# Layer A's Q and K turned by 32x32 block transposes on VectorE instead of 128x128 transposes on TensorE

## The chip, the cores and the metric

One of the eight cores of a Trainium2 chip runs the whole program. The metric is the device time of one execution in microseconds (us). Times of instructions come from the profiled execution. Engines are named as the profile names them: PE is TensorE's matrix multiply, PEld its weight load, DVE is VectorE, ACT is ScalarE, POOL is GpSimd, SP issues DMAs.

## The reference

Four layers in a row, A, B, A, B, on one sequence of 2048 rows of 512, each with a residual and a layer norm ahead of it. The two A layers have the same weights, so have the two B layers.

```python
def _A_ref(x, mem0, Wq, Wk, Wv, Wo, seg_len):      # H = 32 heads of 128, M = 8, seg_len = 32
    mem = mem0
    for s in range(n_seg):                          # 64 segments, one after the other
        h = jnp.concatenate([mem, xs], axis=1)      # 40 rows
        q, k, v = (einsum('btd,dhe->bhte', h, W) for W in (Wq, Wk, Wv))
        scores = einsum('bhqe,bhke->bhqk', q, k) * scale      # masked
        o = einsum('bhqk,bhke->bhqe', softmax(scores), v)
        o = einsum('bhte,hed->btd', o, Wo)
        mem = o[:, :M]                              # the next segment needs it
        outs.append(o[:, M:])
def _B_ref(x, wqkv, wo):                            # full softmax attention, 32 heads of 16, no mask
    ...
x = x + _A_ref(_layernorm(x), ...);  x = x + _B_ref(_layernorm(x), ...)
x = x + _A_ref(_layernorm(x), ...);  x = x + _B_ref(_layernorm(x), ...)
```

The 64 segments of a layer A are a chain, since each needs the memory rows that the one before it made. Layer B is a large amount of work without such a chain.

## The kernel before

**Order of the work.** The Python code that builds the program keeps a clock of its own for PE, ACT and DVE (class `Clock`) and puts TensorE's instructions in order by it: at each step the method `step` takes what can start first of three kinds of work. These are the steps of the present segment of layer A (from a list, `PLAN`, or `PLAN_PAIRS` where at least five units of B are due in the segment; `a_pick` looks at the first six steps left), units of layer B, and chains (layer norm, projections of B, output of B) with planned places `PLACE` and `B_PLACE`. The other engines take their instructions in the order in which a scheduler puts them. Each engine's queue is worked off in order.

**A segment of layer A.** It has 32 main rows (8 memory rows and 24 fresh ones); the 8 remaining fresh rows of four segments are gathered in `a_hX` and go through the projections once for four segments, by the chain in `ln_chunk`. A projection is split into two halves of sixteen heads (`rr`). For a half, `col_steps` issues sixteen matmuls (L737): the 32 rows of `a_hT` are the weights of a 32-column tile of the array, four column tiles stand side by side, each streams 512 columns of W, and the four results lie in the four quarters of a PSUM bank's partitions. Steps `Q0 Q1 K0 K1 V0 V1` are these. For Q and K the bank is copied to SBUF as bf16 (`a_qk`, through `evac`, on ACT or DVE, whichever the clock says ends first). The rows then lie on the partitions, and the scores need the head's 128 elements there. Steps `X0 X1` (Q) and `Y0 Y1` (K) do this turn: four 128x128 transposes on TensorE (L761) into a bank, and a copy of it to `a_QT` or `a_KT` (`evac16`, L335 on ACT, L337 on DVE). For the gathered rows, `turn` in `ln_chunk` does it for K and Q at once, eight transposes from `a_qkx` to `a_KX` and `a_QX`; GpSimd later copies their parts to `a_KT` and `a_QP`. `S0 S1` are the scores (L795, L801), the exponential on ACT (L805), and on DVE the sum, the reciprocal, the product and two 32x32 block transposes (L808 to L817). `P0 P1` or the halves `A`, `B` are the products with V (L824), evacuated to `a_OT`, and `W0` to `W3` the products with Wo (L854), after which DVE writes the next segment's memory rows (L978).

**A unit of layer B** (`emit_qk`, `pv_mm`) is four row-tiled score matmuls of 512 columns (L588), two exponentials on ACT, one of 1536 columns out of the three banks of `b_SX` (L590) and one of 512 out of a fourth bank (L593), and four column-tiled matmuls with V (L602). `b_SX` exists once. How many units go into a segment is the segment's quota: none while there is no backlog, 8 at most, and up to 13 in the last 16 segments. What is left of layer B when the last segment is done is worked off in the tail by `fill` (L473, and L476 on ACT, 1536 columns each).

**Tiling mode.** Matmuls over the full array, row-tiled ones (L588, L824) and column-tiled ones (L737, L795, L801, L602) alternate on TensorE; the builder's clock charges 0.104 us for a change from one to another.

Of the kernel before, what the change touches and what calls it, by code (L numbers as in the profile page):

```python
# [40 lines left out]
PLACE = (-2.0, -1.5, -1.4, -1.4, -1.3, -0.5, -0.4, -0.4, 3.8)  # L41
B_PLACE = (-2.7, -1.4, 0.4, 0.7, 1.7)
# [70 lines left out]
class Kern:  # L113
    def __init__(self, ctx, tc, T):
# [103 lines left out]
    def a_buffers(self, bp):  # L218
# [442 lines left out]
    def ln_chunk(self, A, ck):  # L661
# [30 lines left out]
        qk = {}  # L692

        def one(rr, w):
            def then(b, done):
                t = self.lnp.tile([128, 512], bf16, name="a_qkx", tag="t", bufs=4)
                b.free = self.evac(t[:], b.t[:], 512, done)
                qk[w] = (t, b.free)
            return self.col_steps((self.Wq, self.Wk)[w], lambda ft: self.hX[:, ft, :], rr, max(self.at["x"], self.w_at["QK"[w]]), then)

        def turn(rr):
            b, done = self.turn((qk[1], qk[0]))
            ps = b.h(8, 128)
            self.evac16(self.KX[:, rr].rearrange("p j t q -> p j (t q)"), ps[:, 0:4], 512, done)
            b.free = self.evac16(self.QX[:, 4 * rr:4 * rr + 4].rearrange("p t j q -> p t j q"), ps[:, 4:8].rearrange("p j (t q) -> p t j q", q=32), 512, done)
            if rr:
                self.at["X", ck] = b.free
            return b.free
# [41 lines left out]
    def stage(self, b, done):  # L750
        t = self.stp.tile([128, 512], bf16, name="a_qk")
        b.free = self.evac(t[:], b.t[:], 512, done)
        return t, b.free
# [957 lines left out]
```

## Time and profile before

| | |
|---|---|
| median of 3 runs | 3019.47 us (3016.03 to 3024.8) |
| span of the profiled execution, first to last instruction | 3016.9 us |
| what lies around that span, up to the median of the runs | 2.6 us |
| PE busy | 2793.8 us, 93% of the span |
| ACT busy | 2296.1 us, 76% |
| DVE busy | 1787.0 us, 59% |
| the transposes L761 | 2560 in all, 219.5 us of PE's busy time |

PE's busy time counts a matmul from its start to a modelled end, and matmuls overlap, so a busy PE is not PE at its peak. Where all of PE's instructions follow each other without a gap, the chain of waits gives the time that each group adds.

### The profile page before, as it was taken

How to read it: one execution, taken by the hardware profiler on the slowest of the kernel's cores; microseconds unless marked ns; L12 is line 12 of the kernel's file. 1: busy time of each engine (PE TensorE's matmuls, PEld its weight loads, DVE VectorE, ACT ScalarE, POOL GpSimd, SP SyncE). 2: the span in 40 equal slices, each digit the busy share in tenths (PEclk: the TensorE clock that was granted, in tenths of full speed). 3: DMA queues.
4: the chain of work that ended last, by engine and by line, in shares of the span. 5: the costliest groups of instructions: out<-in, count | busy, mean ns of one | idle time of the engine just before them, and what ended most of it. 6: DMA issues, size and time to landing. Idle time of an engine off the chain costs nothing.

```text
span 3016.9 us, 153258 instructions
## 1 busy us (share of the span) xinstructions
PE 2793.8 (93%) x68190; PEld 1702.6 (56%) x68190; DVE 1787.0 (59%) x4836; ACT 2296.1 (76%) x2816; POOL 661.3 (22%) x1165
## 2 busy tenths in 40 slices
PE   5999999999999999999999999999999999998897
PEld 3666565655555555555656655555556555554463
DVE  2344646476666766577766667767666666654302
ACT  2555767587788788667787777778778899899996
POOL 2222222222222222203212212222222122221110
PEclk9999999999999999999999999999999999999998
DMA  6112224243444446435434433544452544555340
GB/s 255 50 47 77 87 82 122 83 136 114 141 123 142 136 118 192 125 106 171 131 99 123 123 91 116 149 140 129 120 170 81 171 125 131 182 168 159 104 120 14
DMA packets 281282, 373.74 MB, mean 124 GB/s; under 512 B 74105, under 2 KB 202305, under 8 KB 279073
## 3 DMA queue, kind: packets, MB, share of 16 engines
q1 hardware_dynamic: 222096, 186.25, 21.9%
q0 software_dynamic: 55040, 168.68, 17.6%
q8 instruction: 535, 8.77, 1.2%
q10 hardware_dynamic: 3472, 8.91, 0.8%
q14 instruction: 139, 1.13, 0.1%
HBM read 260.06 MB, written 103.55 MB: 121 GB/s over the span
## 4 chain that ended last, share of the span: by engine, by line
PE 62%; ACT 14%; DVE 9%; issue 8%; DMA 6%; POOL 1%; SPq 0%; DVEq 0%; ACTq 0%; POOLq 0%
PE bank L737 23%; PE bank L854 12%; ACT b_pr L476 7%; PE b_SX L588 6%; PE b_oacc L602 6%; PE bank L761 4%; ACT b_pt L590 3%; PE bank L824 3%; DMA b_W<-in_B_wqkv_dram 2%; ACT b_pt L593 2%; PE bank L801 1%; PE bank L1237 1%; PE bank L1283 1%; DMA a_Wq<-in_A_Wq_dram 1%; DVE a_qk L326 1%
## 5 line engine op out<-in xcount | busy, mean ns | idle before, releaser
L590 ACT ACTIVATE b_pt<-b_SX 128x1536 bf16<-128x1536 f32 (+1 forms) x877 | 1270.9, 1449 | 384.3 <-PE bank L588 354.6
L593 ACT ACTIVATE b_pt<-bank 128x512 bf16<-128x512 f32 (+1 forms) x877 | 523.2, 597 | 0.6 <-PE bank L588 0.6
L854 PE MATMUL bank<-a_OT,a_Wo 128*128 128x40 bf16 x16384 | 482.0, 180 | 24.3 <-ACT a_OT L324 18.4
L854 PEld LDWEIGHTS <-a_Wo 128*128 128x128 bf16 x16384 | 449.4, 96 | 67.2 <-issue 58.7
L737 PEld LDWEIGHTS <-a_hT 128*32 128x32 bf16 x12288 | 298.0, 96 | 294.9 <-issue 38.5
L588 PE MATMUL b_SX<-b_q,b_k 32*128 32x256 bf16 (+3 forms) x3870 | 353.0, 313 | 21.1 <-ACT b_pt L590 13.8
L588 PE MATMUL bank<-b_q,b_k 32*128 32x512 bf16 (+3 forms) x1290 | 337.0, 312 | 8.4 <-DVE a_V L326 2.5
L602 PE MATMUL b_oacc<-b_pt,b_v 128*17 128x512 bf16 (+3 forms) x5160 | 322.9, 314 | 11.0 <-DVE b_ain L1070 4.3
L326 DVE CAST a_OT<-bank 128x160 bf16<-128x160 f32 x778 | 216.7, 316 | 127.9 <-PE bank L824 125.1
L737 PE MATMUL bank<-a_Wv,a_hT 128*32 128x512 bf16 x4096 | 285.4, 383 | 1.7 <-DVE b_O L1330 1.3
L326 DVE CAST a_qk<-bank 128x512 bf16<-128x512 f32 x338 | 229.5, 681 | 84.2 <-PE bank L737 79.6
L737 PE MATMUL bank<-a_Wk,a_hT 128*32 128x512 bf16 x4096 | 271.8, 382 | 5.3 <-DVE a_hT L978 5.1
L737 PE MATMUL bank<-a_Wq,a_hT 128*32 128x512 bf16 x4096 | 275.5, 381 | 0.7 <-DVE a_V L326 0.4
L476 ACT ACTIVATE b_pr<-b_S 128x1536 bf16<-128x1536 f32 x202 | 270.9, 1876 | 1.1 <-PE b_S L473 1.1
L588 PEld LDWEIGHTS <-b_k 32*128 32x128 bf16 x5160 | 119.2, 91 | 193.7 <-issue 156.0
L1055 POOL DMA_DIRECT2D b_A<-b_ain x176 | 96.2, 546 | 595.8 <-DVE b_ain L1070 403.1
L1070 DVE TENSOR_TENSOR b_ain<-b_oacc,b_ain 128x512 f32<-128x512 f32 (+1 forms) x244 | 165.6, 679 | 91.9 <-PE b_oacc L602 88.0
L602 PEld LDWEIGHTS <-b_v 128*17 128x17 bf16 x6432 | 117.2, 88 | 163.0 <-issue 125.1
L761 PE MATMUL bank<-c_ident,a_qk 128*128 128x128 bf16 x2048 | 179.9, 221 | 23.1 <-DVE a_qk L326 12.7
L824 PE MATMUL bank<-a_PT,a_V 32*128 32x40 bf16 x3472 | 181.0, 177 | 15.3 <-DVE chk L351 3.4
L761 PEld LDWEIGHTS <-a_qk 128*128 128x128 bf16 x2048 | 119.6, 98 | 123.6 <-DVE a_qk L326 49.9
L808 DVE TENSOR_REDUCE a_sm<-a_pn 128x5 f32<-128x200 bf16 x256 | 92.4, 361 | 161.3 <-ACT a_pn L805 157.6
(156 smaller groups left out, 4103.1 us busy)
## 6 DMA issues: line engine op xcount, KB each, us to landing
b_ain<-b_A SPq DMA_DIRECT2D x232, 256.0 KB
b_W<-in_B_wqkv_dram POOLq DMA_DIRECT2D x192, 256.0 KB, 4.0
b_A<-b_ain POOLq DMA_DIRECT2D x176, 256.0 KB, 3.0
b_q<-b_Q SPq DMA_DIRECT2D x252, 128.0 KB
b_k<-b_K SPq DMA_DIRECT2D x199, 128.0 KB
b_v<-b_V SPq DMA_DIRECT2D x306, 68.0 KB
b_A<-b_aout POOLq DMA_DIRECT2D x80, 128.0 KB, 2.8
a_rest<-a_vx POOLq DMA_DIRECT2D x64, 128.0 KB, 2.7
```

What stands on the lines that cost most here:

```text
L326: self.nc.vector.tensor_copy(dst, src)
L476: nc.scalar.activation(self.ring[:, s:s + n, :], self.sets[i][:, 0:n, :], ACT.Exp, scale=B_SCALE)
L588: nc.tensor.matmul(out[t][:, j * qw:(j + 1) * qw], lhsT=k[32 * t:32 * t + 32, kj * 128:(kj + 1) * 128], rhs=q[32 * t:32 * t + 32, j * u.ru ...
L590: nc.scalar.activation(pt[:, 0:NX, 0:w], self.SX[:, 0:NX, 0:w], ACT.Exp, scale=B_SCALE)
L593: nc.scalar.activation(pt[:, NX + i, 0:w], b.t[:, 0:w], ACT.Exp, scale=B_SCALE)
L602: self.nc.tensor.matmul(self.oacc[32 * t:32 * t + 17, j * step:j * step + qw], lhsT=u.v[:, kj, 17 * t:17 * t + 17], rhs=u.p[:, t, j * qw:( ...
L737: self.nc.tensor.matmul(b.t[32 * t:32 * t + 32, :], lhsT=lhsT(ft), rhs=W[:, ft, n * 512:(n + 1) * 512], start=(ft == 0), stop=(ft == 3), t ...
L761: self.nc.tensor.transpose(ps[:, 4 * i + j, :], x[:, 128 * j:128 * j + 128], self.ident[:])
L824: self.nc.tensor.matmul(ps[:, L * h4:L * h4 + L], lhsT=V[32 * t:32 * t + rows, st, h4 * DH:(h4 + 1) * DH], rhs=self.PT[32 * t:32 * t + row ...
L854: self.nc.tensor.matmul(ps[:, ft, :], lhsT=self.Wo[:, h, 128 * ft:128 * ft + 128], rhs=self.OT[:, h, :], start=(h == 0 and ft == 0), stop= ...
L1055: B.k.nc.gpsimd.dma_start(B.Acc_d[self.qc][self.hg][:, self.qo:self.qo + self.qw], acc[:, 0:self.qw])
L1070: nc.vector.tensor_tensor(acc[:, w], k.oacc[:, w], acc[:, w], ALU.add)
```

## The change

Q and K are no longer turned on TensorE. The projection streams W in another order of columns: a column tile now gets 32 of the 128 elements of each of the sixteen heads of its half, as sixteen runs of 32 columns that lie 128 columns apart (`Wt[:, ft, rr, :, t, :]`), where it got four whole heads as 512 columns in a row. In the bank, each 32x32 block is then one head's rows by 32 of its elements, in the quarter of the partitions where those elements belong. After the copy to `a_qk`, one `nc.vector.transpose` of 128x512 turns all 64 blocks in place of four TensorE transposes and the second copy out of PSUM. V and Wo keep their code.

```diff
-PLACE = (-2.0, -1.5, -1.4, -1.4, -1.3, -0.5, -0.4, -0.4, 3.8)
+PLACE = (-2.1, -1.6, -1.4, -1.1, -0.9, -0.5, -0.4)
...
-        self.QT = bp.tile([128, 2, 4, 4, MAIN], bf16, name="a_QT")
-        self.KT = bp.tile([128, 2, 4, 4, L], bf16, name="a_KT")
+        self.QT = bp.tile([128, 2, 16, MAIN], bf16, name="a_QT")
+        self.KT = bp.tile([128, 2, 16, L], bf16, name="a_KT")
...
         def one(rr, w):
             def then(b, done):
-                t = self.lnp.tile([128, 512], bf16, name="a_qkx", tag="t", bufs=4)
-                b.free = self.evac(t[:], b.t[:], 512, done)
-                qk[w] = (t, b.free)
...
-        def turn(rr):
-            b, done = self.turn((qk[1], qk[0]))
...
+                at = self.turn((self.QX, self.KX)[w][:, rr], b, done)
...
-    def col_steps(self, W, lhsT, rr, ready, then):
+    def col_steps(self, W, lhsT, rr, ready, then, turned=False):
         st = {}
+        Wt = W[:].rearrange("p f (r i t c) -> p f r i t c", r=2, t=4, c=32)
...
-                self.nc.tensor.matmul(b.t[32 * t:32 * t + 32, :], lhsT=lhsT(ft), rhs=W[:, ft, n * 512:(n + 1) * 512],
-                                      start=(ft == 0), stop=(ft == 3), tile_position=(0, 32 * t))
+                out, rhs = b.t[32 * t:32 * t + 32, :], W[:, ft, n * 512:(n + 1) * 512]
+                if turned:
+                    out, rhs = out.rearrange("p (i c) -> p i c", c=32), Wt[:, ft, rr, :, t, :]
+                self.nc.tensor.matmul(out, lhsT=lhsT(ft), rhs=rhs, start=(ft == 0), stop=(ft == 3), tile_position=(0, 32 * t))
...
-    def turn(self, xs):
-        b, at = self.take()
-        ps = b.h(8, 128)
-        for i, (x, _) in enumerate(xs):
-            for j in range(4):
-                self.nc.tensor.transpose(ps[:, 4 * i + j, :], x[:, 128 * j:128 * j + 128], self.ident[:])
+    def turn(self, dst, b, done):
+        x = self.stp.tile([128, 16, 32], bf16, name="a_qk")
+        b.free = self.evac(x[:].rearrange("p i c -> p (i c)"), b.t[:], 512, done)
+        self.nc.vector.transpose(dst, x[:])
+        return self.ck.ew("DVE", 512, b.free)
...
-    PLAN = "K0 Q0 P1 Q1 Y0 X0 S0 W1 K1 W0 Y1 V0 X1 W3 W2 V1 S1 P0".split()
-    PLAN_PAIRS = "W1 Q0 W3 V0 Y0 K0 A1 X0 S0 X1 V1 K1 Q1 B0 Y1 A0 B1 S1 W0 W2".split()
+    PLAN = "W0 K0 Q0 K1 Q1 S0 S1 P0 P1 V0 V1 W2 W1 W3".split()
+    PLAN_PAIRS = "K0 Q0 S0 Q1 B0 V0 A0 K1 S1 A1 W3 V1 W0 W1 B1 W2".split()
```

Since the order on TensorE comes from the builder's clock, all of it moves. Three places in segment 54 (counted from 0; eight units of B) show how. The first is TensorE behind the end of a K projection: before, this is where the four transposes of `a_qk` stand, between the projection (column-tiled) and the scores of a unit (row-tiled).

```order
L737 MATMUL bank0_242<-a_Wk_250,a_hT_253 32x512
L761 LDWEIGHTS a_qk_30069
L761 MATMUL bank3_245<-c_ident_65,a_qk_30069 128x128
L761 LDWEIGHTS a_qk_30069
L761 MATMUL bank3_245<-c_ident_65,a_qk_30069 128x128
L761 LDWEIGHTS a_qk_30069
L761 MATMUL bank3_245<-c_ident_65,a_qk_30069 128x128
L761 LDWEIGHTS a_qk_30069
L761 MATMUL bank3_245<-c_ident_65,a_qk_30069 128x128
L588 LDWEIGHTS b_k_29847
L588 MATMUL b_SX_241<-b_q_29692,b_k_29847 128x256
```

No such rows are left in the changed kernel. Over the whole order before the tail, changes of tiling mode fall from 3109 to 2601, and 22 units of B move from the segments to the tail (7 of them from segments 68 to 111, 14 from the last 16, 1 from segments 64 to 67).

The second place is VectorE in the same segment of the kernel before: the casts of two Q and K halves, the copies out of the banks that TensorE's transposes wrote, and the softmax of a half (L808 to L817).

```order
L326 CAST a_qk_30069<-bank3_245 128x512
L326 CAST a_V_265<-bank1_243 128x512
L326 CAST a_qk_30115<-bank0_242 128x512
L337 COPY a_QT_256<-bank3_245 128x512
L337 COPY a_KT_257<-bank2_244 128x16x32
L326 CAST a_V_265<-bank0_242 128x512
L808 TENSOR_REDUCE a_sm_268<-a_pn_262 128x5
L811 RECIPROCAL a_r_30203<-a_sm_268 128x5
L813 TENSOR_TENSOR a_pn_262<-a_pn_262,a_r_30203 128x5x40
L815 STREAM_TRANSPOSE a_PT_264<-a_pn_262 128x4x2x32
L817 STREAM_TRANSPOSE a_PT_264<-a_pn_262 128x2x4x8
```

In the changed kernel VectorE's queue has the new transposes (L746) there, most of them behind their own cast.

```order
L746 STREAM_TRANSPOSE a_KT_257<-a_qk_28971 128x16x32
L326 CAST a_qk_29001<-bank1_243 128x512
L746 STREAM_TRANSPOSE a_QT_256<-a_qk_29001 128x512
L326 CAST a_qk_29020<-bank3_245 128x512
L746 STREAM_TRANSPOSE a_QT_256<-a_qk_29020 128x512
L326 CAST a_V_265<-bank2_244 128x512
L784 TENSOR_REDUCE a_sm_268<-a_pn_262 128x5
L787 RECIPROCAL a_r_29099<-a_sm_268 128x5
L789 TENSOR_TENSOR a_pn_262<-a_pn_262,a_r_29099 128x5x40
L791 STREAM_TRANSPOSE a_PT_264<-a_pn_262 128x4x2x32
L793 STREAM_TRANSPOSE a_PT_264<-a_pn_262 128x2x4x8
L746 STREAM_TRANSPOSE a_KT_257<-a_qk_29120 128x16x32
```

The last row turns `a_qk_29120`, whose cast is not on VectorE. It stands on ScalarE, the third place, where before this segment had exponentials alone.

```order
L593 ACTIVATE b_pt_29031<-bank1_243 128x512
L781 ACTIVATE a_pn_262<-bank0_242 128x5x40
L324 CAST a_qk_29120<-bank3_245 128x512
L590 ACTIVATE b_pt_29127<-b_SX_241 128x1536
L593 ACTIVATE b_pt_29127<-bank1_243 128x512
```

Of the 640 new transposes, 353 follow a cast on VectorE and 287 wait for one on ScalarE. Casts of other tiles go from VectorE to ScalarE too: 74 of `a_OT` (160 columns) and 77 of `a_V`.

## Rows read from the trace of the kernel before

**Rows 1.** The page, busy us, share and instructions of each engine.
```profile
PE 2793.8 (93%) x68190; PEld 1702.6 (56%) x68190; DVE 1787.0 (59%) x4836; ACT 2296.1 (76%) x2816; POOL 661.3 (22%) x1165
```

**Rows 2.** The page, shares of the chain that ended last.
```profile
PE 62%; ACT 14%; DVE 9%; issue 8%; DMA 6%; POOL 1%; SPq 0%; DVEq 0%; ACTq 0%; POOLq 0%
```

**Rows 3.** Windows: stretch, us, busy PE, PEld, DVE, ACT, POOL, PEclk, DMA, GB/s.
```profile
101.00:281.40 180.40, 168.40 (x5014) 115.01 (x5011) 75.30 (x240) 94.14 (x210) 41.97 (x72) 0.99 0.19 56
281.40:641.60 360.20, 341.76 (x9106) 214.87 (x9103) 211.60 (x590) 244.41 (x371) 87.09 (x151) 1.00 0.34 100
641.60:1227.20 585.60, 559.63 (x14059) 335.03 (x14055) 402.68 (x1065) 469.79 (x563) 146.67 (x258) 0.99 0.46 137
1227.20:1375.20 148.00, 133.96 (x2546) 80.71 (x2542) 92.26 (x253) 88.37 (x111) 25.02 (x44) 0.95 0.40 118
1375.20:2319.30 944.10, 905.00 (x23255) 552.85 (x23253) 650.88 (x1746) 739.07 (x885) 219.77 (x384) 0.99 0.43 127
2319.30:2700.20 380.90, 358.87 (x8381) 204.51 (x8377) 244.42 (x631) 339.12 (x386) 87.63 (x154) 0.99 0.49 148
2700.20:3016.90 316.70, 261.59 (x4145) 158.37 (x4140) 81.50 (x212) 287.14 (x220) 35.64 (x63) 0.97 0.37 109
```

**Rows 4.** Windows of L854 alone: stretch, us, busy PE (matmuls), PEld, PEclk, DMA.
```profile
641.60:1227.20 585.60, 104.50 (x3591) 97.90 (x3587) 0.99 0.46 137
1375.20:2319.30 944.10, 166.95 (x5635) 154.42 (x5633) 0.99 0.43 127
2319.30:2700.20 380.90, 63.53 (x2057) 56.37 (x2053) 0.99 0.49 148
```

**Rows 5.** Groups of PE by line: busy us, mean ns, idle before.
```profile
L761 PE MATMUL bank<-c_ident,a_qk 128*128 128x128 bf16 x2048 | 179.9, 221 | 23.1 <-DVE a_qk L326 12.7 <-DVE a_xo L1204 5.3 <-ACT a_QX L335 3.4
L761 PE MATMUL bank<-c_ident,a_qkx 128*128 128x128 bf16 x512 | 39.6, 220 | 0.9 <-ACT a_qkx L324 0.7 <-issue 0.2
```

**Rows 6.** The chain in 1000 to 1026 us: start, us, what.
```profile
1007.54 0.33 PE bank L761 x4
1007.88 0.98 PE bank L737 x16
...
1008.94 0.23 PE bank L801 x32
...
1012.96 0.55 PE bank L761 x8
```

**Rows 7.** Groups of DVE by form: busy us, mean ns, idle before.
```profile
L326 DVE CAST a_qk<-bank 128x512 bf16<-128x512 f32 x338 | 229.5, 681 | 84.2 <-PE bank L737 79.6 <-ACT b_pt L590 0.2
...
L815 DVE STREAM_TRANSPOSE a_PT<-a_pn 128x256 bf16<-128x256 bf16 x256 | 113.7, 444 | 7.9
...
L337 DVE COPY a_QT<-bank 128x512 bf16<-128x512 bf16 x223 | 92.3, 414 | 4.1 <-ACT b_pt L593 3.0 <-PE bank L761 0.6
L817 DVE STREAM_TRANSPOSE a_PT<-a_pn 128x64 bf16<-128x64 bf16 x256 | 51.7, 202 | 0.0
```

**Rows 8.** Groups of ACT by form: busy us, mean ns, idle before.
```profile
L324 ACT CAST a_qk<-bank 128x512 bf16<-128x512 f32 x174 | 102.6, 590 | 58.1 <-PE bank L737 57.9
...
L324 ACT CAST a_OT<-bank 128x160 bf16<-128x160 f32 x90 | 26.0, 306 | 32.6 <-PE bank L824 32.6
```

**Rows 9.** Timeline of ACT at 2559 us: start, us, line, op, what.
```profile
2559.18 1.45 ACT L590 ACTIVATE b_pt<-b_SX 128x1536 bf16<-128x1536 f32 x1 [0.54 <-PE bank L588]
2560.53 0.59 ACT L593 ACTIVATE b_pt<-bank 128x512 bf16<-128x512 f32 x1
2561.18 1.45 ACT L590 ACTIVATE b_pt<-b_SX 128x1536 bf16<-128x1536 f32 x1
```

**Rows 10.** Source L476, the exponentials of the tail: durations, first and last start.
```profile
L476 ACT ACTIVATE b_pr<-b_S x202: 1283/1908/2139, 2720.9 to 2990.9; 128x1536 bf16<-128x1536 f32 x101
```

**Rows 11.** Waits for Q and K casts: us in total, times, longest us.
```profile
PEld L761 <- DVE a_qk L326: 49.9, 131, 1.7
PEld L761 <- ACT a_qk L324: 11.4, 28, 0.8
```

More of the change, by code (lines that the diff above doesn't have):

```diff
@@ L691, in rest @@
             return self.col_steps(self.Wv, lambda ft: self.hX[:, ft, :], rr, self.w_at["V"], then)
-        qk = {}
         def one(rr, w):
             def then(b, done):
-                t = self.lnp.tile([128, 512], bf16, name="a_qkx", tag="t", bufs=4)
-                b.free = self.evac(t[:], b.t[:], 512, done)
-                qk[w] = (t, b.free)
-            return self.col_steps((self.Wq, self.Wk)[w], lambda ft: self.hX[:, ft, :], rr, max(self.at["x"], self.w_at["QK"[w]]), then)
-        def turn(rr):
-            b, done = self.turn((qk[1], qk[0]))
-            ps = b.h(8, 128)
[L704 to L708, printed above, removed]
+                at = self.turn((self.QX, self.KX)[w][:, rr], b, done)
+                if rr and w:
+                    self.at["X", ck] = at
+            return self.col_steps((self.Wq, self.Wk)[w], lambda ft: self.hX[:, ft, :], rr, max(self.at["x"], self.w_at["QK"[w]]), then, turned=True)
         plan = [4 * ck + x for x in PLACE] if ck else ()
         v = [lambda: rest(0), lambda: rest(1)]
-        x = [lambda: one(0, 0), lambda: one(0, 1), lambda: turn(0), lambda: one(1, 0), lambda: one(1, 1), lambda: turn(1)]
-        c = self.chain([pe] + (x + v if late else v + x), self.ck.t["PE"] + wait, modes="fccfccfcc" if late else "fccccfccf", plan=plan, gate=(6, 4 * ck - 1))
-        c.v_left = 1 if late else 7
+        x = [lambda: one(0, 0), lambda: one(0, 1), lambda: one(1, 0), lambda: one(1, 1)]
+        c = self.chain([pe] + (x + v if late else v + x), self.ck.t["PE"] + wait, modes="fcccccc", plan=plan, gate=(4, 4 * ck - 1))
+        c.v_left = 1 if late else 5
         return c
@@ L748, in cols @@
         return out
[L750 to L753, printed above, removed]
-    def turn(self, xs):
-        b, at = self.take()
-        ps = b.h(8, 128)
-        for i, (x, _) in enumerate(xs):
-            for j in range(4):
-                self.nc.tensor.transpose(ps[:, 4 * i + j, :], x[:, 128 * j:128 * j + 128], self.ident[:])
-        return b, self.ck.pe(0.224 * len(xs), max([at] + [r for _, r in xs]), "full", 4 * len(xs))
+    def turn(self, dst, b, done):
[3 more added lines that the diff above has]
+        return self.ck.ew("DVE", 512, b.free)
     def qk_steps(self, h_s, proj, rr):
         def then(b, done):
-            self.staged["QK"[proj], rr] = self.stage(b, done)
-        return self.col_steps((self.Wq, self.Wk)[proj], lambda ft: h_s[:, ft, :], rr, max(self.at.get("mem", 0.0), self.w_at["QK"[proj]]), then)
-    def qk_turn(self, proj, rr):
-        b, done = self.turn([self.staged["QK"[proj], rr]])
-        ps = b.h(8, 128)[:, 0:4]
-        if proj:
-            dst, src = self.KT[:, rr, :, :, 0:MAIN], ps.rearrange("p j (t q) -> p j t q", q=MAIN)
-        else:
-            dst, src = self.QT[:, rr].rearrange("p j t q -> p j (t q)"), ps
-        b.free = self.at["X", proj, rr] = self.evac16(dst, src, 512, done)
+            self.at["X", proj, rr] = self.turn((self.QT[:, rr], self.KT[:, rr, :, 0:MAIN])[proj], b, done)
+        return self.col_steps((self.Wq, self.Wk)[proj], lambda ft: h_s[:, ft, :], rr, max(self.at.get("mem", 0.0), self.w_at["QK"[proj]]), then, turned=True)
     def v_steps(self, h_s, rr):
@@ L887, in a_ready @@
         return max(t, self.bank_at())
-    MODE = {"Q": "PV", "K": "PV", "X": "full", "Y": "full", "S": "PV", "V": "PV", "P": "S", "A": "S", "B": "S", "W": "full"}
+    MODE = {"Q": "PV", "K": "PV", "S": "PV", "V": "PV", "P": "S", "A": "S", "B": "S", "W": "full"}
     def a_pick(self, left):
@@ L928, in segment @@
         self.at["VR"] = self.at["R"] = INF
-        self.staged = {}
         wo = None
```

27 lines of the change are left out of this document (10 added, 17 removed).

## The prediction

> **What bounds the kernel now.** The page comes first: TensorE is busy 93% of the span, ScalarE 76%, VectorE 59% [rows 1], and the chain that ended last runs through TensorE for 62% and through ScalarE for 14% [rows 2]. That is an average, so the windows come next, cut where the load changes. A segment issues 128 matmuls with Wo, so the counts of L854 say how many segments a stretch holds: 28, 44 and 16 in the three stretches shown [rows 4]. I speak of five stages [rows 3]. *Early* is the time up to 641.6 us, 36 segments with few units of B or none; in its shown part TensorE is busy 93 to 95%, ScalarE 52 to 68%, VectorE 42 to 59%. *Middle* is 641.6 to 1227.2 and 1375.2 to 2319.3, 72 segments, most with eight units: together 1529.7 us, 21.25 a segment, TensorE 95.7%, ScalarE 79.0%, VectorE 68.9%. Between them lies the *change of layers*, 4 segments, TensorE 90.5%. *Late* is 2319.3 to 2700.2, 16 segments of 23.8 us, TensorE 94.2%, but ScalarE 89.0%. In the *tail* ScalarE has 90.7% and TensorE 82.6%. So TensorE binds up to 2319 us, TensorE and ScalarE together after that, and ScalarE alone in the tail. The third view is the chain in a packed stretch, which says what a group adds where TensorE never waits: four transposes 0.33 us, eight 0.55 [rows 6]. The four more cost 0.22, so a transpose costs 0.055 and the change of tiling mode ahead of them 0.11. A projection's sixteen matmuls take 0.98, less the 0.11 that is 0.22 for a group of four.
>
> **What TensorE loses.** All 2560 transposes go [rows 5], 20 a segment: 2560 x 0.055 = 141 us. Changes of mode before the tail fall by 508: 508 x 0.11 = 56 us. The 22 units that move to the tail have two groups of four each: 22 x 0.44 = 10 us. Sum 207 us. By stage: early 720 transposes and 89 changes, 50; middle 1440, 309 and 7 units, 116; change of layers 80, 15 and a unit, 7; late 320, 96 and 14 units, 34. L761's busy time, 179.9 + 39.6 = 219.5, is of the same size.
>
> The Trainium skill (VectorE: DVE Perf Modes, The three transpose paths) gives 390 ns for a 128x128 transpose on TensorE and 311 on VectorE. By that, as an estimate, 640 turns of four would free 998 us of TensorE and the time would be near 2,060. The rows disagree, since L761 holds 219.5 us in all, and they decide.
>
> **What the projections of Q and K may gain or lose.** Their streams are now sixteen runs of 32 columns instead of one of 512, in 10,240 matmuls, 2560 groups of four. No row of before shows such a stream. From below I price it at nothing: no fewer columns are streamed, so a gain is excluded. From above by the shortest streams in the chain, L801's 40 columns: 32 matmuls, eight groups, in 0.23 us, 0.029 a group [rows 6]; sixteen of these are 0.46 against 0.22, so at most 0.24 a group more, 614 us in all. I take nothing, because L737's price per column is set by the count of columns, which stays, and because the L801 row has a weight load for each 40 columns, which a run has not.
>
> The Trainium skill (SBUF — State Buffer, Specifications (TRN2)) says that SBUF is read in lines of 16 bytes and needs two hits a line for its full rate. A run of 64 bytes has eight a line, so by that page the price is nothing too; no run here shows it yet.
>
> **What VectorE gets.** The trace has block transposes of 256 and of 64 elements, 444 and 202 ns [rows 7]: 1.26 ns an element, so 512 take 0.77 us, which I take. The bounds are a 512-element bf16 copy, 0.41, and twice the 256-element row, 0.89. 640 x 0.77 = 493 us. Away go 556 copies out of the banks at 0.415, 231 us, and casts that move to ScalarE (74 of 160 columns at about 0.31, 126 of 512 at 0.68), 109 us. Net +153: 1787 becomes 1940, 66% of the time forecast, 69% at the upper bound. VectorE doesn't become the bound. The way from a projection to the scores stays as long: cast 0.68, transposes 0.33, copy 0.41 are 1.42; cast and turn are 1.45.
>
> **What ScalarE gets.** In the middle its copies and casts of 512 rise from 101 to 187, 86 x 0.59 = 51 us, those of 160 by 44, 14 us [rows 8], and 7 units of 1.45 + 0.59 [rows 9] leave, 14 us. So 1208.9 becomes 1260, 17.5 us a segment. Late it is 12 casts of 512 and 14 of 160 more and 14 units fewer: 339 becomes 322, 20.1 a segment.
>
> **How much of TensorE's time becomes span.** Early, both other engines have room; I count nine tenths of 50, 45 us, the rest for places where the scores wait for a turn. In the middle the two ends are these. If ScalarE reached the 89% that it has late, a segment would last 17.5 / 0.89 = 19.7 us, just what TensorE's saving alone allows (21.25 less 116/72 = 19.6), and all 116 us would be saved. If it stayed at 79%, 17.5 / 0.79 = 22.2, nothing would. I take 86%, nearer to the late stage, because there too TensorE has little more to do than ScalarE; but below it, because the added casts come when a projection ends, and then hold up the next unit's exponentials, which own the only `b_SX`. The timeline shows what that is worth even without a cast: 2.00 us from one unit to the next, after an idle 0.54 [rows 9]. 17.5 / 0.86 = 20.3, 0.95 x 72 = 68 us. Late, ScalarE stays at 89%: 20.1 / 0.89 = 22.6, 1.2 x 16 = 19 us. Change of layers: 5 of 7. Sum 137 us.
>
> **What comes back in the tail.** 22 units are 88 tiles of 512, 29.3 exponentials of three tiles, which follow each other at (2990.9 - 2720.9) / 201 = 1.343 us [rows 10]: +39 us on the engine that binds there.
>
> Net 137 - 39 = 98: the span goes from 3016.9 to 2919, and with the 2.6 us by which the median of the runs lies above that span, to **2922 us**.
>
> **Rivals.**
> *All of it is saved.* For it: TensorE at 95% over 2200 us, and ScalarE's 89% late. 207 - 39 = 168, 2852 us. Against it: no stage has TensorE at 95.7% and ScalarE at 89% at once.
> *ScalarE holds its share and the middle saves nothing.* For it: the casts go to the fuller engine. 45 + 5 + 19 - 39 = 30, about 2990 us.
> *The streams in runs are dear.* Then TensorE binds everywhere, and the 168 is set against the price: it decides at 168 / 2560 = 0.066 us a group, 30% of 0.22. At half of the upper bound, +307, the time is 3159 us. For it speaks only that no row excludes it.
> *VectorE's queue stands behind ScalarE.* 287 turns wait for a cast on ScalarE; behind such a turn stand V casts, the softmax and the evacuations of `a_OT`, for which the products with V and Wo on TensorE wait. A cast that comes behind a unit's exponentials is up to 2.04 us late, 1 us in the mean; if half of that reaches TensorE, 287 x 0.5 = 144 us, 3066 us. It decides at 98 / 287 = 0.34 us a turn. Against it: the transposes of before waited 11.4 us in all for 174 casts on ScalarE and 49.9 for 338 on VectorE [rows 8, 11, 7], 0.07 and 0.15 a cast.
>
> **Chances.** The forecast, between 2885 and 2985 us, 0.50; all saved 0.20; the middle saves nothing, between 2985 and 3030, 0.14, of which 0.08 is still faster; streams dear 0.07; VectorE's queue 0.09. A measurement of this kernel tells about 0.3% from no change, 9 us. So faster 0.50 + 0.20 + 0.08 = 0.78, within 0.3% 0.06, slower 0.16. The range from 2835 to 3020 takes in the full saving and ScalarE's case, and leaves out most of the two slow ones.
>
> **What would show it.** In the profile after: no L761; L730 with Wq and Wk at the same mean duration as L730 with Wv (the price of nothing); L746 at 0.77 us; VectorE near 1940 us in sum, ScalarE near 2340; middle segments of 20.3 us with ScalarE at 86%; about 231 exponentials in the tail, and a tail 39 us longer. The prediction is wrong if Wq and Wk matmuls are longer than Wv's, if TensorE's longest waits are for `a_QT`, `a_KT` or `a_PT` from VectorE, or if the middle's TensorE share stays above 95%, which would mean the full saving.

## The result and the profile after

The changed kernel takes 2975.39 us (median of 4 runs, 2972.97 to 2977.35) against 3021.62 us for the kernel before beside it: ratio 0.9842, interval 0.9825 to 0.9859. It is faster by 1.6%, clear of the interval: 46 us where 98 were forecast; 2975 lies within the range of 2835 to 3020. The profiled execution has a span of 2973.5 us and a mean granted clock of 0.959 (before: 3016.9 and 0.987).

The page of the changed kernel, engines and chain; against [rows 1, 2] TensorE's busy time is down by 111.4 us, ScalarE's and VectorE's are up, and the chain lies less on TensorE and more on ScalarE. The chain's share under "issue" (time in which an engine waited for nothing that the profile shows) goes from 8 to 16%, which no run here explains:
```profile
PE 2682.4 (90%) x65827; PEld 1606.8 (54%) x65827; DVE 1869.7 (63%) x4712; ACT 2319.6 (78%) x2923; POOL 665.8 (22%) x1165
...
PE 48%; ACT 20%; issue 16%; DVE 8%; DMA 5%; POOL 3%; SPq 0%; POOLq 0%; ACTq 0%; DVEq 0%
```

Windows of the changed kernel, cut at the ends of the same segments as [rows 3] and with the same columns:
```profile
93.70:259.00 165.30, 151.89 (x4770) 102.56 (x4766) 102.63 (x273) 78.47 (x177) 42.56 (x72) 1.00 0.21 61
259.00:605.10 346.10, 319.45 (x8706) 196.17 (x8702) 235.79 (x597) 237.42 (x363) 86.74 (x150) 0.98 0.35 102
605.10:1180.20 575.10, 534.25 (x13503) 313.01 (x13498) 410.38 (x1012) 484.42 (x614) 147.77 (x257) 0.96 0.47 139
1180.20:1329.20 149.00, 126.80 (x2408) 73.41 (x2405) 90.77 (x239) 88.89 (x118) 23.09 (x41) 0.90 0.38 108
1329.20:2257.50 928.30, 863.80 (x22280) 516.05 (x22276) 661.78 (x1670) 752.38 (x953) 222.71 (x387) 0.96 0.44 129
2257.50:2614.50 357.00, 329.86 (x7888) 187.59 (x7885) 244.11 (x594) 321.84 (x389) 85.46 (x148) 0.95 0.49 149
2614.50:2973.50 359.00, 298.07 (x4674) 179.84 (x4670) 85.33 (x218) 326.26 (x249) 38.99 (x69) 0.96 0.36 106
```

By stage, in us:

| stage | before | after | change | forecast |
|---|---|---|---|---|
| early | 641.6 | 605.1 | -36.5 | -45 |
| middle | 1529.7 | 1503.4 | -26.3 | -68 |
| change of layers | 148.0 | 149.0 | +1.0 | -5 |
| late | 380.9 | 357.0 | -23.9 | -19 |
| tail | 316.7 | 359.0 | +42.3 | +39 |

Four stages are within 9 us of the forecast; the middle is 42 short. There TensorE's busy time fell from 1464.6 to 1398.1 us, by 67 and not by 116, and its idle time rose from 65 to 105 us. The column that has changed beside it is the granted clock: 0.99 before in both parts of the middle, 0.96 after. A mean of 0.959 over 2973.5 us is 2 x 0.041 x 2973.5 = 244 us at the lower of the two levels (1.2 GHz instead of 2.4), against 78 us by the same sum before. I call this the half-clock time; with a clock of three digits it is good to some 3 us.

One place shows how such a stretch begins. Windows and timeline of TensorE in the changed kernel, at the start of segment 48 (windows: the columns as above; timeline: start, us, line, operation, tiles, idle time ahead and what ended it):
```profile
860.00:864.00 4.00, 3.28 (x104) 1.85 (x96) 3.97 (x12) 3.94 (x8) 1.53 (x4) 1.00 0.31 94
864.00:866.00 2.00, 0.00 (x1) 0.01 (x1) 1.11 (x6) 1.62 (x2) 1.96 (x4) 0.83 0.69 242
866.00:869.00 3.00, 3.00 (x50) 1.79 (x51) 1.94 (x8) 1.75 (x2) 0.00 (x0) 0.50 0.02 5
869.00:872.00 3.00, 3.00 (x69) 3.00 (x67) 1.20 (x3) 0.19 (x1) 2.18 (x3) 0.50 0.35 81
872.00:876.00 4.00, 4.00 (x132) 3.29 (x129) 0.94 (x4) 2.89 (x3) 0.12 (x1) 0.98 0.66 209
```
```profile
866.00 0.61 PE L385 MATMUL bank<-c_ident,ln_xn 128*128 128x128 bf16 x4 [2.02 <-DVE ln_xn L378]
...
867.08 1.03 PE L602 MATMUL b_oacc<-b_pt,b_v 128*17 128x256 bf16 x16
...
868.42 1.89 PE L1205 MATMUL bank<-b_hT,b_W 128*128 128x128 bf16 x16
870.11 2.28 PE L830 MATMUL bank<-a_OT,a_Wo 128*128 128x40 bf16 x64
```
TensorE waits 2.02 us for the layer-normed tile of layer B; while it waits the clock falls to 0.50, and it stays there through the 6 us from 866 to 872, in which TensorE is busy without a gap. In all the trace has 42 such stretches, before 16.

TensorE's waits in the changed kernel (us in total, times, longest); the waits of [rows 11] are gone with L761, and others have grown:
```profile
PE b_SX L588 <- ACT b_pt L590: 42.6, 92, 1.6
PE bank L385 <- DVE ln_xn L378: 30.7, 17, 3.0
...
PE bank L777 <- DVE a_QT L746: 10.2, 16, 1.2
```
Before, the first two were 13.8 and 5.1 us.

### The profile page after: what moved, and what is told of

Read it like the earlier page. It is cut to its first block, busy times and chain, and to the rows that moved or that the text cites. A ratio compares the mean times of both kernels' runs of the same rounds, so it can differ in the third digit from the quotient of the medians.

```text
span 2973.5 us, 148030 instructions
## 1 busy us (share of the span) xinstructions
PE 2682.4 (90%) x65827; PEld 1606.8 (54%) x65827; DVE 1869.7 (63%) x4712; ACT 2319.6 (78%) x2923; POOL 665.8 (22%) x1165
## 4 chain that ended last, share of the span: by engine, by line
PE 48%; ACT 20%; issue 16%; DVE 8%; DMA 5%; POOL 3%; SPq 0%; POOLq 0%; ACTq 0%; DVEq 0%
PE bank L730 16%; PE bank L830 12%; ACT b_pr L476 9%; ACT b_pt L590 7%; PE b_SX L588 6%; PE b_oacc L602 4%; ACT b_pt L593 3%; PE bank L800 2%; PE bank L1205 2%; DMA b_W<-in_B_wqkv_dram 2%; DVE a_QT L746 1%; PE bank L777 1%; DVE a_qk L326 1%; PE bank L1251 1%; DMA b_A<-b_ain 1%
## 5 line engine op out<-in xcount | busy, mean ns | idle before, releaser
L590 ACT ACTIVATE b_pt<-b_SX 128x1536 bf16<-128x1536 f32 (+1 forms) x855 | 1241.7, 1452 | 345.7 <-PE bank L588 323.1
L593 ACT ACTIVATE b_pt<-bank 128x512 bf16<-128x512 f32 (+1 forms) x855 | 511.2, 598 | 0.0
L830 PE MATMUL bank<-a_OT,a_Wo 128*128 128x40 bf16 x16384 | 497.9, 182 | 13.9 <-ACT a_OT L324 8.6
L730 PEld LDWEIGHTS <-a_hT 128*32 128x32 bf16 x12288 | 313.5, 96 | 282.9 <-issue 42.1
L588 PE MATMUL b_SX<-b_q,b_k 32*128 32x256 bf16 (+3 forms) x3738 | 350.3, 320 | 50.7 <-ACT b_pt L590 42.6
L588 PE MATMUL bank<-b_q,b_k 32*128 32x512 bf16 (+3 forms) x1246 | 335.4, 319 | 7.8 <-ACT b_pt L593 3.6
L602 PE MATMUL b_oacc<-b_pt,b_v 128*17 128x512 bf16 (+2 forms) x4984 | 317.8, 322 | 5.4 <-DVE b_ain L1038 3.9
L476 ACT ACTIVATE b_pr<-b_S 128x1536 bf16<-128x1536 f32 x231 | 310.0, 1919 | 0.6 <-PE b_S L473 0.6
L326 DVE CAST a_OT<-bank 128x160 bf16<-128x160 f32 x704 | 195.6, 314 | 179.3 <-PE bank L800 176.1
L588 PEld LDWEIGHTS <-b_k 32*128 32x128 bf16 x4984 | 118.8, 92 | 256.9 <-issue 228.7
L324 ACT CAST a_qk<-bank 128x512 bf16<-128x512 f32 x287 | 170.0, 593 | 79.6 <-PE bank L730 78.7
L195 POOL DMA_DIRECT2D b_W<-in_B_wqkv_dram x192 | 145.7, 761 | 300.8 <-PE bank L1205 165.4
L746 DVE STREAM_TRANSPOSE a_KT<-a_qk 128x512 bf16<-128x512 bf16 x256 | 179.9, 703 | 48.6 <-ACT a_qk L324 41.4
L800 PE MATMUL bank<-a_PT,a_V 32*128 32x40 bf16 x3448 | 183.9, 178 | 27.2 <-DVE a_xo L1172 5.9
```

Of the source, the lines that this page charges most:

```text
L324: self.nc.scalar.copy(dst, src)
L326: self.nc.vector.tensor_copy(dst, src)
L476: nc.scalar.activation(self.ring[:, s:s + n, :], self.sets[i][:, 0:n, :], ACT.Exp, scale=B_SCALE)
L588: nc.tensor.matmul(out[t][:, j * qw:(j + 1) * qw], lhsT=k[32 * t:32 * t + 32, kj * 128:(kj + 1) * 128], rhs=q[32 * t:32 * t + 32, j * u.ru ...
L590: nc.scalar.activation(pt[:, 0:NX, 0:w], self.SX[:, 0:NX, 0:w], ACT.Exp, scale=B_SCALE)
L593: nc.scalar.activation(pt[:, NX + i, 0:w], b.t[:, 0:w], ACT.Exp, scale=B_SCALE)
```

## Experiments

Three theories went in. **1:** the granted clock falls behind TensorE's new gaps and gives back what was saved. **2:** the waits alone bind, ScalarE's and VectorE's, and the clock costs nothing. **3:** the new order of steps took the gain. e9 is the changed kernel once more, beside e10 to e12:

> The changed kernel once more, unaltered, on the same chip as the three kernels beside it, so that their stages can be set against its stages. Every theory: ratio to the kernel before 0.981 to 0.987.

Each ratio is to the kernel before on the same chip; half-clock time is worked out as above from each run's span and mean clock, TensorE's busy time is the page's (both in us). e1 to e8 were not run beside e9: their times are compared by ratio, and spans and busy times are those of the profiled executions.

| run | ratio (interval) | TensorE busy | half-clock |
|---|---|---|---|
| the change, again (e9) | 0.9846 (0.9825 to 0.9867) | 2686.0 | 244 |
| e1 fill at L385 | 0.9847 (0.9834 to 0.9860) | 2723.1 | 173 |
| e2 layer norm later | 0.9888 (0.9874 to 0.9902) | 2685.2 | 257 |
| e3 dead transposes | 1.0523 (1.0509 to 1.0536) | 2926.1 | 217 |
| e4 old order | 1.0043 (1.0025 to 1.0062) | 2700.4 | 231 |
| e5 all gaps filled | 0.9774 (0.9754 to 0.9794) | 2718.0 | 113 |
| e6 before, new order | 1.0281 (1.0255 to 1.0306) | 2858.2 | 99 |
| e7 transposes twice | 1.0822 (1.0799 to 1.0845) | 2762.5 | 367 |
| e8 casts on VectorE | 1.0113 (1.0094 to 1.0132) | 2724.2 | 330 |
| e10 gaps half filled | 0.9754 (0.9736 to 0.9772) | 2692.2 | 130 |
| e11 no transposes | 0.9721 (0.9698 to 0.9743) | 2662.4 | 206 |
| e12 casts on ScalarE | 1.0146 (1.0127 to 1.0166) | 2728.0 | 271 |

**e1, the wait at L385 filled.**
```diff
     def transposes(self, xn, dst, ready=0.0, warm=0):
         b, at = self.take()
+        for _ in range(warm):
+            self.nc.tensor.matmul(b.t[:, 0:128], lhsT=self.ident[:], rhs=self.ident[:], start=True, stop=True)
...
-            return k.transposes(st["xn"], lambda ps: nc.vector.tensor_copy(k.hB[:], ps))
+            return k.transposes(st["xn"], lambda ps: nc.vector.tensor_copy(k.hB[:], ps), warm=32)
```


> The changed kernel, with 32 small matmuls (the identity by itself, 128 columns each, some 0.056 us each, 1.8 us together) ahead of the four transposes of the layer-normed tile that layer B projects, on a bank already taken: they wait for nothing, so TensorE works through what was its idle time at that place (31.9 us before L385 in the changed kernel, 11 of its waits of some 2 us in the middle stages). The order of all other instructions stays. Theory 1 (the granted clock: TensorE, lighter now, idles for 1 to 2.5 us at such places, and the rows show it at 1.2 GHz for 3.4 or 6.8 us behind them, 126 us in the two middle stages against 19 in the kernel before): the time at half clock in the middle stages falls from 126 us to under 80, and although 57 us of work are added the time comes out at 2945 to 2972 us. Theory 2 (the waits alone bind, the lower clock costs nothing because TensorE would wait anyway): the half-clock time may fall, the time does not, 2970 to 3005 us, the added work where it doesn't fit into idle time. Theory 3 (the new order of steps took the gain): no view, 2975 to 3000.

Half-clock time fell by 71 us, the wait at L385 from 30.7 to 4.8 us, and the time stayed: 2986, in the range of theory 2 and outside that of theory 1. The sums of the profiled executions say why. The fill (1024 small matmuls, at all 32 places, where the change has 17 waits) took 74.5 us of TensorE; all its other work took 37 us less than in e9 (2686.0 to 2648.6), and idle time fell by 22 (290.0 to 267.8). So the other work did get shorter, as theory 1 has it, but the fill cost more than that and the idle time that it took up; the time alone does not exclude theory 2.

**e2, the layer norm given more time.**
```diff
-            return b.free + 2.8
+            return b.free + 4.6
```


> The changed kernel, with the builder's estimate of the layer norm's latency ahead of layer B's projections raised from 2.8 to 4.6 us, so that the four transposes at L385 are placed later among TensorE's instructions and other work stands in the gap. No work is added or left out. Theory 1: the idle time before L385 falls from 31.9 us to under 12, the half-clock time of the middle stages from 126 us to under 90, and the time to 2935 to 2962 us. Theory 2: the idle time goes to other places (the wait for ScalarE at L588 and the sums at L800), half-clock time with it, the time stays within 0.3%, 2966 to 2984 us. Theory 3 (the order of steps): changes by up to 15 us either way.

Slower, 0.9888 for 0.9842, some 14 us: against theories 1 and 2, and within the 15 us either way of theory 3. The wait left L385 (30.7 to 2.8 us) and went to other places, as theory 2 has it, and grew there (L588 from 42.6 to 60.7 us, L800 for `a_PT` from 5.6 to 12.1); half-clock time did not fall. Waits of TensorE in this run:
```profile
PE b_SX L588 <- ACT b_pt L590: 60.7, 114, 1.6
...
PE bank L800 <- DVE a_PT L793: 12.1, 15, 1.3
...
PE bank L385 <- DVE ln_xn L378: 2.8, 1, 2.8
```

**e3, the removed TensorE work put back as dead work.** Four transposes of the identity into each Q and K bank, overwritten by the column matmuls.
```diff
+            if turned and ft == 0:
+                for i in range(4):
+                    self.nc.tensor.transpose(b.h(4, 128)[:, i, :], self.ident[:], self.ident[:])
             for t in range(4):
```


> The changed kernel with as many transposes on TensorE as the kernel before had, as dead work: four transposes of the identity (some 0.055 us each) into each of the 640 banks of layer A's Q and K columns ahead of the first column matmul, whose start overwrites them; nothing waits for them and nothing reads them. The order of all else stays, VectorE's transposes too. 141 us of work are added at full clock, and some 66 us more if each unit pays two mode changes of 0.05 us. This measures what TensorE's removed time is worth in the changed kernel. Theory 1 (half of what was removed was lost to the lower clock and to waits): the half-clock time of the middle stages falls back from 126 us to under 50, and the time rises by only 60 to 110 us, 3035 to 3085 us. Theory 2 (waits for ScalarE and VectorE bind now; TensorE has room): rises by under 45 us, to 2990 to 3020. If TensorE bound it fully and the clock gave nothing back: plus 140 to 200 us, 3115 to 3175.

TensorE got 240 us of work and the span 218 us (3193.6 against 2976.0 in e9), more than any of the three ranges. The 240 are more than the transposes alone, since this order has 1115 changes of tiling mode more (3208 become 4323, counted in the traces): 141 us and 1115 x 0.11, an estimated 264 in all. TensorE's idle time takes in little of it (290 us become 267), so TensorE's time binds here nearly microsecond for microsecond, and theory 2 falls in the form that TensorE has room for such work. One doubt stays: the dead work stands ahead of the projections, on the way to the scores, and would lengthen that way too. Theory 1 was wrong in one point: with all that work back the half-clock time is still 217 us, 130 of it in the middle by the trace's clock records, where under 50 were expected. So a smaller sum of work is not what brings the clock down here; e5 and e10 below try the gaps.

**e4 and e6, order and transposes apart.** e4: the change with the old tables. e6: the kernel before with the new ones, the transposes' steps put between projection and scores.
```diff
-    PLAN = "W0 K0 Q0 K1 Q1 S0 S1 P0 P1 V0 V1 W2 W1 W3".split()
+    PLAN = "K0 Q0 P1 Q1 S0 W1 K1 W0 V0 W3 W2 V1 S1 P0".split()
```
```diff
-    PLAN = "K0 Q0 P1 Q1 Y0 X0 S0 W1 K1 W0 Y1 V0 X1 W3 W2 V1 S1 P0".split()
+    PLAN = "W0 K0 Q0 Y0 X0 K1 Q1 S0 Y1 X1 S1 P0 P1 V0 V1 W2 W1 W3".split()
```


> The changed kernel with the order tables of the kernel before: its two lists of steps with the eight entries of the transposes taken out, its places for the chunk's chain without the two transposes, and its places for layer B's tile. Transposes stay on VectorE. Theory 3 (the new order and places cost what is missing): faster by 15 to 45 us, 2930 to 2960. Theory 1: within 15 us either way, 2960 to 2995, with the half-clock time of the middle stages again over 90 us, since the lighter TensorE and not the order makes the gaps. Theory 2: the same range, without a view on the clock.

> The kernel before, transposes on TensorE, with the changed kernel's order of steps: its two lists with the eight entries of the transposes put between each projection and the scores that need it, its places for layer B's tile and for the chunk's chain. It tells whether the new order has a worth of its own, after the changed kernel in the old order was 1.0043 of the kernel before. If order and transposes are separate gains (the order worth 2% anywhere): ratio 0.975 to 0.987. If the new order is worth something only where the transposes stand on VectorE (there it gives the longer way from a projection to its scores time to pass): 0.995 to 1.015. If the old order was the better one for transposes on TensorE: over 1.015.

Theory 3 falls, with its sign turned round: transposes on VectorE in the old order gain nothing (1.0043, outside the ranges of all three theories), the new order with transposes on TensorE loses 2.8%, both together gain 1.6%. In e6 TensorE is busy for 64 us more than before [rows 1]. The trace has 316 changes of tiling mode more (3639 become 3955), an estimated 35 us at the prediction's 0.11; the rest is open. The places of the transposes in e6's lists are one choice of many.

**e5 and e10, the gaps filled.** A table, made from the trace of the changed kernel, says ahead of which step how many small matmuls go into the bank that the step has already taken; no other instruction moves.
```diff
+    def fill_gap(self, line, n, b):
+        at = self.seen.get(line, 0)
+        self.seen[line] = at + n
+        for _ in range(GAPS.get((line, at), 0)):
+            self.nc.tensor.matmul(b.t[:, 0:128], lhsT=self.ident[:], rhs=self.ident[:], start=True, stop=True)
```


> The changed kernel with small matmuls (the identity by itself, some 0.056 us each) at those places where its trace shows TensorE idle for over 0.4 us, as many at each as fit into the idle time less 0.25 us: 1103 of them at some 85 places, 62 us together. They go into the bank that the waiting step has already taken and wait for nothing else; the order of all other instructions stays, and where the estimate of the idle time holds, nothing starts later. So this changes the granted clock and little else. Theory 1 (the clock): the time at half clock, 241 us in all in the changed kernel and 78 in the kernel before, falls below 150 us, TensorE's rows are shorter for it, and the time falls by a third to a half of the microseconds that go back to full clock: ratio to the kernel before 0.960 to 0.977 (the changed kernel had 0.984). Theory 2 (the waits bind and the clock costs nothing): half-clock time falls as well, but the ratio stays at 0.981 to 0.990.

> The filled kernel with half of the fill: 560 small matmuls in place of 1103, at the places with over 0.6 us of idle time, for the idle time less 0.5 us at 0.07 us each (that is what one took in the filled kernel's trace, not 0.056) and at most 24 at a place. In the filled kernel the clock gave back 27 us in the middle, but its small matmuls took 53 us there and the idle time fell by only 25. Theory 1 (clock): the same return of clock at less price, half-clock time below 170 us in all, ratio 0.968 to 0.979. Theory 2 (the filled kernel's gain came by chance of order or placement): no gain over the changed kernel, 0.980 to 0.988. If the clock needs the whole gap filled: half-clock time near 200 us and ratio 0.978 to 0.984.

Both came out as theory 1 has it, e5 at the very edge of its range (0.9774 for at most 0.977). e10 is a faster kernel than the change: 0.9754 against 0.9846 in e9 beside it, intervals apart, 0.92% of 3037.6 us = 28 us. The same place in e10, TensorE's timeline:
```profile
864.55 1.35 PE L584 MATMUL bank<-c_ident 128*128 128x128 bf16 x21
866.62 0.40 PE L399 MATMUL bank<-c_ident,ln_xn 128*128 128x128 bf16 x4 [0.73 <-DVE ln_xn L391]
...
867.28 0.62 PE L623 MATMUL b_oacc<-b_pt,b_v 128*17 128x256 bf16 x16
...
868.14 1.05 PE L1233 MATMUL bank<-b_hT,b_W 128*128 128x128 bf16 x16
869.03 1.76 PE L857 MATMUL bank<-a_OT,a_Wo 128*128 128x40 bf16 x64
```
and the windows there:
```profile
864.00:867.00 3.00, 2.26 (x50) 1.78 (x48) 2.11 (x12) 2.26 (x5) 2.58 (x6) 1.00 0.68 221
867.00:870.00 3.00, 3.00 (x96) 2.52 (x96) 2.41 (x9) 1.94 (x2) 0.95 (x2) 1.00 0.14 39
```
The layer-normed tile is no earlier, but the clock stays at 1.00. From L399 to the end of L857 it takes 869.03 + 1.76 - 866.62 = 4.17 us, the same instructions in the changed kernel 870.11 + 2.28 - 866.00 = 6.39: one fall cost 2.2 us, 2.22 / 6.39 = 0.35 us for each microsecond at half clock. Over the whole span the sums agree. The fill's rows and the middle's windows of e10:
```profile
L584 PE MATMUL bank<-c_ident 128*128 128x128 bf16 x560 | 48.1, 240 | 15.3 <-ACT b_pt L614 6.3 <-DVE b_xo L1368 5.4 <-DVE b_hT L1207 2.3
```
```profile
608.40:1174.50 566.10, 536.00 (x13674) 316.42 (x13669) 410.15 (x1012) 484.88 (x614) 147.40 (x257) 0.99 0.49 141
1323.50:2247.60 924.10, 864.71 (x22503) 519.57 (x22500) 660.90 (x1669) 752.93 (x953) 222.72 (x387) 0.98 0.45 130
```
Without the fill TensorE is busy for 2692.2 - 48.1 = 2644.1 us, 42 us less than e9 for the same instructions; 114 us fewer at half clock, by 0.35, make 40. Not all of the 42 show in the time, because the fill doesn't lie wholly in idle time: of its 48.1 us the idle time took in 21 (290.0 to 269.0), so in these two executions the span falls by 42 - 27 = 15 us (2976.0 to 2961.2). The other runs of e9 were slower than its profiled one, hence the 28 by the medians. e5, with twice the fill, got about as much.

**e7 and e11, VectorE's price from both sides.** e7 makes each transposition twice. e11 leaves it out: Q and K stay unturned, so layer A's scores are of the wrong numbers.
```diff
         self.nc.vector.transpose(dst, x[:])
+        self.nc.vector.transpose(dst, x[:])
```
```diff
-        x = self.stp.tile([128, 16, 32], bf16, name="a_qk")
-        b.free = self.evac(x[:].rearrange("p i c -> p (i c)"), b.t[:], 512, done)
-        self.nc.vector.transpose(dst, x[:])
+        b.free = self.evac(dst, b.t[:].rearrange("p (i c) -> p i c", c=32), 512, done)
```


> The changed kernel with each of the 640 transposes on VectorE made twice, one right behind the other, into the same place: 640 x 0.70 = 449 us more for VectorE, whose share rises from 63% to about 75%; the order of all else stays. It measures what VectorE's time on the way from a projection to its scores is worth. Theory 1 (TensorE's own time and its clock are what counts, VectorE's work is beside it): ratio to the kernel before 0.985 to 1.000, that is at most 45 us of the 449. The rival from the prediction (VectorE's queue, on which the casts and the layer norm stand behind the transposes, sets the waits): 1.005 to 1.05, and the idle times of TensorE before the scores L777, the sums L800 and the layer-normed tile L385 grow by a third or more.

> The changed kernel with VectorE's 640 transposes left out: the cast goes straight into the place where the transposed columns would stand, so Q and K stay unturned and layer A's scores are of the wrong numbers. 640 x 0.70 = 449 us are taken from VectorE; the order of everything stays, and TensorE does the same. It is the other side of the run in which each was made twice (that cost 9.8%, 297 us for 449 us). If what was added there was beyond a threshold and the order leaves room for one transposition (the order was made for it): the time falls by under 30 us, ratio 0.974 to 0.985. If VectorE's work on the way from projection to scores costs per microsecond here too: ratio 0.90 to 0.96, and the idle time of TensorE in the middle (105 us) falls by half. Theory 1 alone: half-clock time falls with the idle time.

One transposition costs (0.9846 - 0.9721) x 3037.6 / 640 = 0.06 us of the time each, 38 us together, a little more than the 30 expected where the order leaves room for one. A second one costs (1.0822 - 0.9846) x 3029 / 640 = 0.46 us each, at 68% VectorE, beyond the ranges of theory 1 and of the rival. The order leaves room for one: TensorE's wait for `a_QT` is 10.2 us with it and in e7
```profile
PE bank L778 <- DVE a_QT L747: 139.6, 135, 2.5
```
So VectorE isn't beside the path; it was just within its slack. In e11 the half-clock time is still 206 us and 53 us of waits at L588 are left: the transposes don't make most of the gaps. Of e11's 38 us TensorE's busy time makes 24 (2686.0 to 2662.4), at 38 us less half-clock time.

**e8 and e12, the casts all on one engine.** The last argument of `evac` for `a_qk` is `"DVE"` in e8 and `"ACT"` in e12.
```diff
-        b.free = self.evac(x[:].rearrange("p i c -> p (i c)"), b.t[:], 512, done)
+        b.free = self.evac(x[:].rearrange("p i c -> p (i c)"), b.t[:], 512, done, "ACT")
```


> The changed kernel with the casts that lead to these transposes all on VectorE (about half of them stand on ScalarE now), so that no transpose waits for ScalarE and ScalarE loses some 0.59 us for each. The builder's order follows from its own cost figures and moves a little. Theory 2 in its form that ScalarE binds the middle (81 to 90% busy there): the waits before L588 shorten, ratio to the kernel before 0.965 to 0.980. Theory 1: ScalarE isn't what TensorE's busy time waits for; VectorE becomes the later one, ratio 0.982 to 1.000.

> The mirror of the run with these casts all on VectorE (ratio 1.011): all casts that lead to the transposes on ScalarE. VectorE, 62 to 68% busy in the early segments with ScalarE at 48 to 69%, loses some 0.68 us for each cast that moves. If the way over VectorE (cast, transposition, softmax, layer norm in one queue) sets TensorE's waits: the early stages (segments 4 to 35) get 5 to 25 us shorter, the late one (ScalarE 90%) longer by up to 10, ratio 0.972 to 0.986. If ScalarE sets them (theory 2): the middle and late stages get 20 us or more longer, ratio 0.988 to 1.01.

Either way costs 2.7 to 3.0%, more than any theory gave. The middle, by windows of e12:
```profile
620.40:1221.80 601.40, 545.71 (x13502) 320.42 (x13499) 338.01 (x909) 528.84 (x716) 146.45 (x256) 0.95 0.46 132
1371.70:2337.20 965.50, 878.25 (x22277) 518.83 (x22274) 548.25 (x1502) 825.07 (x1118) 220.67 (x386) 0.96 0.43 124
```
ScalarE has 117 us more than after, and the middle is 64 us longer; TensorE's wait at L588 for its exponentials is 101.7 us, after the change 42.6. In e8 the early stage (segments 4 to 35) is 45 us longer, where VectorE goes from 66 to 72%. Both engines stand close behind TensorE, and the mixture of the change is better than either end. The builder's order moves with the casts, so part of this is the order; that was not separated.

## Why the prediction was right in direction and wrong in size

- **The streams in runs cost nothing.** This was the largest unknown, and these rows of the page settle it, 8192 of the 10,240 matmuls with Wq and Wk in sixteen runs, at 380 and 381 ns, against Wv's with a single one, at 381 ns:
```profile
L730 PE MATMUL bank<-a_Wv,a_hT 128*32 128x512 bf16 x4096 | 286.2, 381 | 5.2 <-ACT b_pt L593 3.3
...
L730 PE MATMUL bank<-a_Wk,a_hT 128*32 128x512 bf16 x4096 | 277.7, 381 | 7.5 <-DVE a_hT L946 6.0
L730 PE MATMUL bank<-a_Wq,a_hT 128*32 128x512 bf16 x4096 | 277.9, 380 | 0.0
```
  The Trainium skill's rule of lines and hits (SBUF — State Buffer, Specifications (TRN2)) had said the same, and these rows agree. The 3159 us rival falls.
- **VectorE's transposition** takes 0.70 us, not 0.77 (0.703 in this row); VectorE's sum is 1870, not 1940, ScalarE's 2320, not 2340.
```profile
L746 DVE STREAM_TRANSPOSE a_KT<-a_qk 128x512 bf16<-128x512 bf16 x256 | 179.9, 703 | 48.6 <-ACT a_qk L324 41.4
```
- **The tail** was right in both numbers: 231 exponentials as forecast, +42 us for +39.
```profile
L476 ACT ACTIVATE b_pr<-b_S 128x1536 bf16<-128x1536 f32 x231 | 310.0, 1919 | 0.6 <-PE b_S L473 0.6
```
- **What TensorE loses: the step that failed.** The prediction took 207 us off TensorE ahead of the tail, 116 of it in the middle, and left all its other work at the clock of before (0.99 in [rows 3]); a change of the clock was priced at nothing, without a reason. Ahead of the tail TensorE's busy time went from 2793.8 - 261.6 = 2532.2 to 2682.4 - 298.1 = 2384.3 us: 148, which is 59 short. In the middle it is 67 for 116, 49 short, where the time is 42 short. The half-clock time ahead of the tail rose from 58 to 215 us (by the clock records of the two traces), by 157, and at the 0.35 measured at one place that is an estimated 55 us of longer matmuls. The products with Wo, the same 16,384 matmuls, show it in the pages of before, after and e10:
```profile
L854 PE MATMUL bank<-a_OT,a_Wo 128*128 128x40 bf16 x16384 | 482.0, 180 | 24.3 <-ACT a_OT L324 18.4
...
L830 PE MATMUL bank<-a_OT,a_Wo 128*128 128x40 bf16 x16384 | 497.9, 182 | 13.9 <-ACT a_OT L324 8.6
...
L857 PE MATMUL bank<-a_OT,a_Wo 128*128 128x40 bf16 x16384 | 486.0, 180 | 21.2 <-issue 10.9
```
  e10 gave 42 us of TensorE's time back by nothing but fill in the gaps, and its kernel is 28 us faster. So what stayed ran slower. In the middle the half-clock time rose from 19 to 126 us, an estimated 37 of the 49 us that are missing there; the other 12 stay open.
- **How much becomes span** was right in sum and right only in part of its reason. Of the saving 70 us were to turn into idle time, and idle time ahead of the tail rose from 168.0 to 230.2, by 62; in the middle by 40, where 48 were forecast. But the middle's ScalarE didn't reach 86%: it is at 82% (1236.8 of 1503.4), and a segment takes 20.9 us instead of 20.3. The wait that it named, L588's for ScalarE's exponentials, grew by 29 us; the 26 us more at L385, for the layer-normed tile, it did not have. So 62 for 70 is in part luck. In e3 the idle time hardly shrinks under 240 us of added work: it is made of waits for the other engines and is no store that TensorE's work fills.
- **The way from a projection to its scores "stays as long"** (1.42 against 1.45) was right only in the new order, and dear at its edge: 0.06 us a turn, 38 us, was priced at nothing (e11), and the same transposes in the old order leave no gain at all (e4). The rival of VectorE's queue, 0.5 us a turn, was wrong for the kernel as it is and would be right for one more such operation (e7, 0.46).
- **The change of layers** lost 1 us instead of saving 5, with the clock at 0.90 where it was 0.95.

What stays open: which edit makes the gaps. Half-clock time is over 200 us in the changed kernel, with dead TensorE work (e3), in the old order (e4) and without the transposes (e11), and 78 and 99 with transposes on TensorE. e5 and e10 tie it to the gaps; no run ties the gaps to one step. Nor do the prices add up to one sum: the 38 us of e11 hold 24 that are TensorE's shorter work.

## What to carry to other kernels

When work is taken off the engine that binds, price what is left at the clock that it will be granted: look for the places where that engine will now wait a microsecond or two, as at 864 us, and what follows them. Small matmuls that wait for nothing, into a bank that is taken anyway, bought part of that clock back and were worth their price where they were cut to the gap (e5, e10), not where they stood at every place (e1); moving the wait elsewhere (e2) did neither. A moved operation and the order it needs are one change: measured apart, each of the two lost.

## What the runs showed that was not expected

The clock fell again and again in stages in which TensorE is 92 to 93% busy. In 31 of the 42 falls the longest wait just ahead was one of 0.9 to 2.5 us, as at 864 us; a stretch at half clock lasted 244 / 42 = 5.8 us in the mean. Not every such wait did it: of 57 of that length in the trace, 31 had a fall close behind. The Trainium skill (TensorE: Matmul & The Clock Gate, A second HAM failure mode: psum-queue depth-cycling) tells of a kernel in which short idle times between groups of matmuls, often repeated, make the clock go to and fro; the trace agrees in that the clock goes down and up again 42 times. Work at half clock is not twice as long: 64 matmuls with Wo of 40 columns took 2.28 us for 1.76, 16 projections of layer B 1.89 for 1.05. And a small matmul of fill took 48.1 / 560 = 0.086 us where it stood in e10 and 74.5 / 1024 = 0.073 in e1, not the 0.056 taken for it. Whether 560 (0.9754) are better than 1103 (0.9774) is not shown: the intervals overlap.
